# A decayed recurrence and routed attention on one core: small copies on ScalarE and GpSimd, and a new table of order, buffers and engines

## The chip, the cores and the metric

The kernel runs on 1 core of one Trainium2 chip. The metric is the device time in microseconds (us); lower is better. Engines are named as in the profile: PE is TensorE, DVE is VectorE, ACT is ScalarE, POOL is GpSimd, SP is SyncE, which issues every transfer (DMA) of this kernel.

## The reference

Four batches, 8 heads, 768 time steps, head width 48. A linear recurrence with a complex decay runs over time; its output, 384 wide per step, goes through four experts' causal attention, of which each step uses its two best.

```python
mag = np.sqrt(a_re * a_re + a_im * a_im)
scale = np.minimum(mag, 0.999) / (mag + 1e-06)
a_re_n, a_im_n = (a_re * scale, a_im * scale)
for t in range(S):
    new_re = ar * S_re - ai * S_im
    new_im = ar * S_im + ai * S_re
    kv = np.einsum('bhd,bhe->bhde', k[:, :, t], v[:, :, t])
    S_re, S_im = (new_re + kv, new_im)
    y[:, :, t] = np.einsum('bhd,bhde->bhe', q[:, :, t], S_re)
...
logits = x @ w_gate                      # x is y with its heads side by side
topk = np.argpartition(-logits, K, axis=-1)[..., :K]        # K = 2 of 4
w = np.exp(sel); w /= w.sum(-1, keepdims=True) + 1e-09
for e in range(E):
    q, k, v = x @ wq[e], x @ wk[e], x @ wv[e]
    scores = np.where(causal, -1e9, scale * (q @ k.transpose(0, 2, 1)))
    a = np.exp(scores - scores.max(-1, keepdims=True))
    a /= a.sum(-1, keepdims=True) + 1e-09
    ye = a @ v @ wo[e]
    out += mask[..., None] * w[:, :, kk:kk + 1] * ye        # for both chosen kk
```

## The kernel before, in words

The recurrence is done in chunks of 128 steps, 6 to a batch. Two chunks make a piece (256 steps), 3 to a batch, and the decay of a piece is worked out for all 384 features at once, in tiles of 128 partitions by 3 x 256 columns. For a piece, `logs` turns the magnitude into a running sum of logarithms (ACT logarithms and exponentials, DVE products and running sums, the "scans"), `atan` and `angles` do the same for the phase (its running sum goes on from the piece before through a small tile `carry`), `sincos` takes sine and cosine, and `products` multiplies q and k by them. For the very first piece, `groups` cuts this in three thirds of 128 x 256, so that each works while the next is loaded. `regroup` then moves the products by 10 transfers into `fm`, where the heads lie apart: heads 0 to 3 need the first 5 of the 10, heads 4 to 7 the last 5 or 6.

For each chunk PE makes the causal products `psc` (masked by DVE into `pts`), transposes k (`pk`, copied to `kts`), the state's increment `pu` (scaled into `tst`), and the output `yu` (copied to `x`). After two chunks `proj` multiplies x by the weights (`pp`), `vproj` makes values and logits (`pv`, `lg`), and `maxpass` takes row maxima (`pm`). When a batch's six chunks are done, `gate` picks the experts, `score` makes scores `pss` and their exponentials `pe` (POOL masks the diagonal blocks with affine_select), `av` multiplies by the values (`po`) and adds up the exponentials on DVE or POOL, `norm` divides (`dn`, `cb`, `ot`), and `wo` projects to the output (`pw`, `ob`). PE thus works on the scores of one batch while the recurrence of the next is prepared.

`record` lists all operations, 0 to 1875, without running them. The numbers below are places in that list. A table decides the rest: `ORDER` is the order in which they are issued, and so each engine's queue; `HOME` names operations that go to another engine than the one written (a ScalarE copy as `tensor_copy`, Square as a product, Abs as a bit mask, by `moved`); `ROOMS` says which buffer each tile gets; `FILL` puts so many filler matmuls ahead of an operation on PE. A filler multiplies the tile `keep` by itself into the bank that the operation will overwrite; it computes nothing and waits for nothing but `keep` and that bank. Line 860 is the filler's line, line 871 the line that issues all other operations, line 869 ACT's table load: ACT holds one set of functions at a time, one for sine and arctangent, one for logarithm and exponential, and a load stands wherever the order changes between them.

Operations that the prediction speaks of, all of batch 0: 7 makes `keep`; 33 to 35 load the three thirds of the first piece's decay, 118 and 119 the two halves of the second piece's (121 is the first ACT operation on it); 100 to 105 are the sines of the first piece, 106 to 117 its 12 products; 186 to 195 its `fm` transfers, 152 and 153 the decay of the third piece; 200 and 202 the two `psc` of the first chunk (heads 0 to 3 and 4 to 7), 197 and 199 its `kts` copies, 204 its `pu`; 221 to 223 the second chunk's `yu`; 228 and 231 the first two projections; 269 and 283 are third- and fourth-chunk work (`pu` and a `psc`).

```python
for i in ORDER or range(len(plan.ops)):
    if i in FILL:
...
        for _ in range(FILL[i]):
            nc.tensor.matmul(z, real(plan.busy), real(plan.busy)[:, None, :].to_broadcast([128, 4, 128]),
                             start=True, stop=True)
```

Of the kernel before, what the change touches and what calls it, by code (L numbers as in the profile page):

```python
# [26 lines left out]
C2 = 2 * C  # L27
# [15 lines left out]
HOME = {26: 'gpsimd',  # L43
 32: 'gpsimd',
 40: 'vector',
 48: 'vector',
 70: 'vector',
 89: 'vector',
 97: 'vector',
 124: 'vector',  # L50
 134: 'vector',
 145: 'vector',
 150: 'gpsimd',
 169: 'gpsimd',
 183: 'gpsimd',
 199: 'vector',
 208: 'vector',
 213: 'vector',
 220: 'gpsimd',
 287: 'gpsimd',  # L60
 296: 'vector',
 303: 'vector',
 340: 'gpsimd',
 353: 'vector',
 424: 'gpsimd',
 437: 'gpsimd',
 459: 'gpsimd',
 473: 'gpsimd',
 497: 'gpsimd',
# [3 lines left out]
 549: 'gpsimd',  # L73
 551: 'gpsimd',
 563: 'gpsimd',
 571: 'gpsimd',
 583: 'gpsimd',
# [4 lines left out]
 599: 'gpsimd',  # L82
 605: 'gpsimd',
 617: 'gpsimd',
 619: 'gpsimd',
 630: 'gpsimd',
 631: 'gpsimd',
 632: 'gpsimd',
 751: 'vector',
 779: 'vector',  # L90
 781: 'vector',
 788: 'gpsimd',
 867: 'gpsimd',
 880: 'gpsimd',
 907: 'gpsimd',
 926: 'gpsimd',
 943: 'gpsimd',
 945: 'gpsimd',
 953: 'gpsimd',
 960: 'vector',  # L100
 961: 'gpsimd',
 963: 'vector',
 966: 'vector',
 975: 'vector',
 985: 'gpsimd',
 996: 'vector',
 1013: 'gpsimd',
 1030: 'gpsimd',
 1031: 'gpsimd',
 1033: 'gpsimd',  # L110
 1039: 'gpsimd',
 1041: 'vector',
 1044: 'gpsimd',
 1046: 'gpsimd',
 1065: 'gpsimd',
 1067: 'gpsimd',
 1080: 'gpsimd',
 1109: 'vector',
 1116: 'gpsimd',
 1135: 'vector',  # L120
 1167: 'gpsimd',
 1174: 'vector',
 1176: 'vector',
 1183: 'gpsimd',
 1187: 'vector',
 1192: 'vector',
 1199: 'vector',
 1201: 'vector',
 1227: 'vector',
 1240: 'vector',  # L130
 1313: 'gpsimd',
 1320: 'gpsimd',
 1328: 'gpsimd',
 1337: 'gpsimd',
 1339: 'gpsimd',
 1345: 'gpsimd',
 1347: 'gpsimd',
 1354: 'vector',
 1367: 'gpsimd',
 1369: 'gpsimd',  # L140
 1374: 'gpsimd',
 1381: 'vector',
 1382: 'gpsimd',
 1387: 'gpsimd',
 1399: 'gpsimd',
 1409: 'gpsimd',
 1411: 'vector',
 1420: 'vector',
# [3 lines left out]
 1478: 'gpsimd',  # L152
 1479: 'gpsimd',
 1481: 'gpsimd',
 1493: 'gpsimd',
 1494: 'gpsimd',
 1495: 'gpsimd',
 1501: 'gpsimd',
 1512: 'vector',
# [6 lines left out]
 1564: 'gpsimd',  # L166
 1579: 'vector',
 1580: 'vector',
 1583: 'vector',
 1608: 'vector',  # L170
 1619: 'vector',
 1622: 'vector',
 1624: 'vector',
 1640: 'vector',
 1643: 'vector',
 1647: 'vector',
 1708: 'vector',
 1709: 'vector',
 1712: 'vector',
 1761: 'gpsimd',  # L180
 1763: 'gpsimd',
 1776: 'gpsimd',
 1835: 'gpsimd',
 1856: 'vector',
 1857: 'gpsimd'}

FILL = {202: 141, 204: 14, 206: 1, 210: 7, 357: 3, 406: 2, 1873: 4}

ROOMS = {'ab': [0, 1, 0, 1, 0, 1, 0, 1, 0, 1, 0, 1],
 'carry': [0, 3, 2, 3, 2, 1, 1, 3, 1, 2],  # L190
 'fm': [0, 1, 0, 1, 0, 1, 0, 1, 0, 1, 0, 1],
# [30 lines left out]

ORDER = [13, 35, 20, 0, 34, 14, 19, 33, 15, 6, 17, 118, 1, 2, 4, 18, 3, 5, 8, 119, 9, 12, 21, 120, 22, 67, 36, 68, 185, 52, 69, 53, 70, 154, 37, 54, 71, 7,
# [160 lines left out]
def record(ak, vk, w, out):  # L384
    p = Plan()
    V, G = "vector", "gpsimd"
# [4 lines left out]
    ab, fm, vt, xk, qka, v2, lgs, mrow, mx, ot = ({} for _ in range(10))  # L391
# [263 lines left out]
    def gate(b):  # L655
        lg = lgs[b]
# [273 lines left out]
```

## Time and profile before

| what | value |
|---|---|
| median of 3 runs (lowest, highest) | 414.89 us (413.98, 415.06) |
| the profiled execution | 413.87 us, its span 412.2 us |
| PE busy | 398.0 us, 97% of the span |
| DVE, ACT, POOL busy | 346.3 (84%), 280.3 (68%), 157.5 us (38%) |
| granted PE clock, mean | 0.996 of full speed |
| DMA | 53.40 MB moved, 130 GB/s in the mean |

The span runs from the first to the last instruction of one execution; 1.67 us of that execution's time lies around it. A busy PE may be busy with fillers. Queues of the engines run in order: an instruction that waits holds everything behind it on its engine.

### The profile page before, as it was taken

The page shows a single profiled execution, that of the slowest core. Times are in us where ns is not written, and L with a number is a line of the kernel's source. Part 1 is how long each engine was busy: PE and PEld are TensorE (multiplying, and loading weights), DVE is VectorE, ACT ScalarE, POOL GpSimd, SP SyncE. Part 2 cuts the span into 40 slices and gives each one's busy share as a digit, 9 for nine tenths or more (in the row PEclk, how much of TensorE's full clock was granted, in tenths as well). Part 3 has the DMA queues.
Part 4 walks back from the last instruction along what each step waited for, and adds up shares of the span by engine and source line. Part 5 has one row for each costly group of instructions (what it writes and reads, how often), then busy time and mean ns, then how long its engine had stood idle before and what let it go on. Part 6 is the DMA issues. An engine that isn't in the chain of part 4 may idle for free. (4 is left out here: it accounts for less than half of the span.)

```text
span 412.2 us, 9649 instructions
## 1 busy us (share of the span) xinstructions
PE 398.0 (97%) x3792; PEld 326.9 (79%) x3792; DVE 346.3 (84%) x738; ACT 280.3 (68%) x436; POOL 157.5 (38%) x146
## 2 busy tenths in 40 slices
PE   4999799999999999999999999999999999999996
PEld 1445579998888779989887789989779789887775
DVE  5997979999999999999999898798794556978751
ACT  6979788986898898879688999733533222124572
POOL 0002233559373444563263324640166634002440
PEclk9999989999999999999999999999999999999999
DMA  7767808875946506828424703628003510111002
GB/s 266 281 158 202 231 0 214 231 218 132 342 117 190 154 37 164 233 63 269 126 71 116 212 3 116 191 76 233 9 2 76 165 27 2 38 45 54 2 13 103
DMA packets 27261, 53.40 MB, mean 130 GB/s; under 512 B 3536, under 2 KB 7376, under 8 KB 27216
## 3 DMA queue, kind: packets, MB, share of 16 engines
q1 hardware_dynamic: 27216, 52.78, 44.2%
q8 instruction: 30, 0.49, 0.5%
q14 instruction: 15, 0.12, 0.1%
HBM read 26.74 MB, written 4.72 MB: 76 GB/s over the span
## 5 line engine op out<-in xcount | busy, mean ns | idle before, releaser
L871 POOL TENSOR_TENSOR qk<-qk,ab 128x768 f32<-128x768 f32 x20 | 40.0, 2011 | 64.2 <-DVE qk L871 49.1
L871 ACT ACTIVATE pe<-pss 128x1024 f32<-128x1024 f32 (+2 forms) x48 | 43.4, 915 | 26.0 <-PE pss L871 22.4
L871 POOL TENSOR_SCALAR_AFFINE_SELECT pe<-pe 128x256 f32<-128x256 f32 x48 | 25.3, 544 | 84.8 <-ACT pe L871 54.8
L871 PE MATMUL pp<-x,whi 128*128 128x256 f32 x288 | 55.6, 287 | 0.1
L871 PE MATMUL psc<-fm 96*128 96x128 f32 x384 | 52.1, 281 | 0.2
L871 PEld LDWEIGHTS psc<-fm 96*128 96x128 f32 x384 | 46.6, 192 | 3.2 <-issue 0.9
L871 ACT ACTIVATE ab<-ab 128x768 f32<-128x768 f32 (+1 forms) x61 | 45.8, 762 | 4.3 <-DVE ab L871 3.2
L871 PEld LDWEIGHTS pp<-x,whi 128*128 128x128 f32 x288 | 45.4, 189 | 1.5 <-issue 1.5
L871 ACT ACTIVATE qk<-qk 128x768 f32<-128x768 f32 (+3 forms) x64 | 43.1, 684 | 4.0 <-DVE qk L871 3.6
L871 PE MATMUL pss<-qka 64*128 64x256 f32 (+3 forms) x480 | 45.5, 301 | 0.1
L871 PE MATMUL po<-pe,v 128*64 128x256 f32 (+3 forms) x320 | 42.8, 395 | 0.8 <-POOL pe L871 0.8
L869 ACT ACT_TABLE_LOAD x33 | 42.3, 1283 | 1.3 <-PEq L919 0.8
L871 POOL TENSOR_TENSOR pe<-pe 128x512 f32<-128x512 f32 (+2 forms) x25 | 31.7, 1267 | 28.6 <-DVE pe L871 13.3
L860 PEld LDWEIGHTS <-keep 128*128 128x128 bf16 x172 | 17.2, 102 | 29.8 <-issue 6.8
L871 PEld LDWEIGHTS pss<-qka 64*128 64x128 f32 x480 | 35.7, 185 | 6.2 <-issue 2.4
L871 PE MATMUL pp<-x,wlo 128*128 128x256 f32 x144 | 40.3, 280 | 0.0
L860 PE MATMUL psc<-keep 128*128 128x512 bf16 x141 | 32.9, 398 | 6.0 <-DVE keep L871 6.0
L871 DVE TENSOR_TENSOR pts<-psc,keep 128x512 f32<-128x512 f32 x48 | 32.3, 682 | 5.3 <-PE yu L871 2.9
L871 POOL TENSOR_TENSOR qk<-qk 128x768 f32<-128x768 f32 x16 | 25.8, 1620 | 23.6 <-ACT qk L871 23.4
L871 DVE CUSTOM_DVE_ANT_0 junk<-pm,negm 128x128 bf16<-128x128 f32 (+3 forms) x64 | 31.1, 485 | 3.3 <-PE pm L871 2.1
L871 PEld LDWEIGHTS po<-pe,v 128*64 128x64 f32 x320 | 20.7, 136 | 14.9 <-issue 5.0
L871 PE MATMUL pv<-whi,x 128*128 128x260 f32 x144 | 31.1, 292 | 0.0
(121 smaller groups left out, 930.6 us busy)
## 6 DMA issues: line engine op xcount, KB each, us to landing
fm<-qk SPq DMA_DIRECT2D x72, 192.8 KB, 4.7
qk<-in_ak_dram SPq DMA_DIRECT2D x12, 768.0 KB, 5.7
ab<-in_ak_dram SPq DMA_DIRECT2D x22, 384.0 KB, 4.0
vt<-in_vk_dram SPq DMA_DIRECT2D x12, 512.0 KB, 5.9
out_dram<-ob SPq DMA_DIRECT2D x24, 192.0 KB, 1.9
fm<-qk SPq DMA_DIRECT2D x24, 128.5 KB, 4.1
x<-x SPq DMA_DIRECT2D x24, 96.0 KB, 3.0
fm<-qk SPq DMA_DIRECT2D x24, 64.2 KB, 4.2
```

The lines of the kernel that those rows point to most:

```text
L860: nc.tensor.matmul(z, real(plan.busy), real(plan.busy)[:, None, :].to_broadcast([128, 4, 128]), start=True, stop=True)
L869: nc.scalar.preload_act_table_set(need)
L871: getattr(getattr(nc, engine), name)(*a, **k)
```

## The change

Two lines of code move small copies that carry a result on: the end of a piece's phase (`carry`, 10 copies of 128 x 1 or 128 x 3) and the middle part of the gate's coefficients (`cft`, 4 copies of 24 x 128). Both were written for VectorE; they are now ScalarE copies, of which `HOME` sends two `carry` copies to GpSimd.

All four tables are new. `HOME` has other entries: besides the copies, 37 products, sums and splits go from POOL to DVE and 29 from DVE to POOL; copies out of PSUM and within SBUF change between DVE and ACT in both directions (`kts`: 10 from DVE to ACT, 3 back; `x`: 4 and 1). `ORDER` is another order throughout, and with it the number of ACT table loads is 29 (before: 33). `ROOMS` follows it. `FILL` has 185 fillers (before: 172): 130 (141) ahead of the first `psc`, 48 (22) more up to the second chunk's `pu`, and 7 (9) later.

```diff
-HOME = {26: 'gpsimd',
- 32: 'gpsimd',
+HOME = {32: 'gpsimd',
  40: 'vector',
- 48: 'vector',
+ 55: 'vector',
+ 63: 'gpsimd',
...
-FILL = {202: 141, 204: 14, 206: 1, 210: 7, 357: 3, 406: 2, 1873: 4}
+FILL = {200: 130, 202: 17, 204: 14, 206: 6, 218: 3, 221: 8, 288: 2, 406: 3, 1870: 2}
...
-ORDER = [13, 35, 20, 0, 34, 14, 19, 33, 15, 6, 17, 118, 1, 2, 4, 18, 3, 5, 8, 119, 9, 12, 21, 120, 22, 67, 36, 68, 185, 52, 69, 53, 70, 154, 37, 54, 71, 7,
+ORDER = [20, 33, 14, 19, 34, 0, 7, 35, 9, 6, 118, 119, 23, 36, 185, 154, 37, 38, 22, 52, 39, 53, 40, 120, 121, 4, 54, 250, 55, 41, 67, 42, 56, 2, 11, 68, 57,
...
         if k + 1 < NK:
             c = p.tile([128, 3], F32, "carry")[:, :len(js)]
-            p.put(V, "tensor_copy", c, A[:, :, C2 - 1])
+            p.copy(c, A[:, :, C2 - 1])
...
         p.tt(V, r, z, cft[:n], OP.subtract)
-        p.put(V, "tensor_copy", cft[32:32 + n], r)
+        p.copy(cft[32:32 + n], r)
```

First place: the start of DVE's queue, where `keep`, for which the first filler waits, is made. Before, 13 setup operations and three of the decay stood ahead of it:

```order
L871 TENSOR_SCALAR pickneg<-pickneg 128x6
L871 MEMSET col 128x1
L871 MEMSET cmask 128x2
L871 MEMSET negm 128x192
L871 TENSOR_SCALAR negm<-iota 128x128
L871 CAST pick<-ident 24x24
L871 TENSOR_TENSOR ab<-ab 128x256 x3
L871 TENSOR_SCALAR keep<-iota 128x128
```

and of the change, from the first row of the queue:

```order
L908 UNCONDITIONAL_BRANCH
L853 TENSOR_SCALAR keep<-iota 128x128
L853 TENSOR_SCALAR negm<-iota 128x128
L853 TENSOR_SCALAR ident<-iota 128x128
L853 TENSOR_TENSOR ab<-ab 128x256 x2
L853 MEMSET cmask 128x256
```

`keep` is now the first thing that DVE makes (POOL's `iota`, which it reads, has moved behind two small POOL operations).

Second place: the start of ACT's queue, `ab_63` and `qk_102` (`qk_84` in the change) being the first piece's tiles and `ab_80` (`ab_79`) the second piece's. Before, from its third operation:

```order
L871 ACTIVATE qk_102<-ab_63 128x256
L871 ACTIVATE ab_63<-qk_102 128x256
L871 ACTIVATE qk_102<-ab_63 128x256 x2
L871 ACTIVATE ab_63<-ab_63 128x256
L871 ACTIVATE ab_63<-qk_102 128x256
L871 ACTIVATE qk_102<-qk_102 128x256
L871 ACTIVATE qk_102<-ab_63 128x256
L871 ACTIVATE qk_102<-qk_102 128x256
L871 ACTIVATE qk_98<-ab_80 128x3x256
```

and of the change, from its first:

```order
L853 ACTIVATE qk_84<-ab_63 128x256
L853 ACTIVATE ab_63<-qk_84 128x256
L853 ACTIVATE qk_84<-ab_63 128x256
L853 ACTIVATE ab_63<-qk_84 128x256
L853 ACTIVATE qk_99<-ab_79 128x3x256
L853 ACTIVATE qk_84<-ab_63 128x256 x3
L853 ACTIVATE ab_63<-qk_84 128x256
```

The second piece's operation 121 stands after 4 ACT operations on the first piece instead of after 11.

Third place: DVE's queue from the first chunk's `pts` to the second chunk's. Before:

```order
L871 COPY kts<-pk 128x384
L871 SCALAR_TENSOR_TENSOR qk<-qk 128x3x256
L871 SCALAR_TENSOR_TENSOR ab<-col,carry,ab 128x256 x3
L871 SCALAR_TENSOR_TENSOR qk<-qk 128x3x256
L871 SCALAR_TENSOR_TENSOR qk<-cmask,qk 128x256 x3
L871 TENSOR_TENSOR ab<-ab 128x768
L871 SCALAR_TENSOR_TENSOR ab<-ab 128x768
L871 TENSOR_TENSOR tst<-pu,fm 96x384
L871 TENSOR_TENSOR pts<-psc,keep 128x512
L871 CAST x<-yu 128x4x128
L871 TENSOR_TENSOR pts<-psc,keep 128x512
L871 COPY kts<-pk 128x384
```

and of the change:

```order
L853 SCALAR_TENSOR_TENSOR qk<-qk 128x3x256
L853 MEMSET negm 128x192
L853 SCALAR_TENSOR_TENSOR qk<-cmask,qk 128x256 x3
L853 TENSOR_TENSOR ab<-ab 128x768
L853 TENSOR_TENSOR pts<-psc,keep 128x512
L853 TENSOR_TENSOR x<-yu,x 128x4x128
L853 TENSOR_TENSOR tst<-pu,fm 96x384
L853 SCALAR_TENSOR_TENSOR ab<-ab 128x768
L853 TENSOR_TENSOR qk<-qk 128x3x256
L853 TENSOR_TENSOR pts<-psc,keep 128x512
L853 SCALAR_TENSOR_TENSOR qk<-qk 128x3x256
L853 TENSOR_TENSOR wlo<-wst,whi 128x768
```

The two `kts` copies and the `x` copy have left DVE for ACT, and one `pts` and the state's `tst` stand ahead of the phase's `ab` operation instead of behind it.

## Rows read from the trace of the kernel before

**Rows 1.** The page's part 1: busy us, share of the span and instructions of each engine.

```profile
PE 398.0 (97%) x3792; PEld 326.9 (79%) x3792; DVE 346.3 (84%) x738; ACT 280.3 (68%) x436; POOL 157.5 (38%) x146
```

**Rows 2.** Stretches: length, busy us of PE, PEld, DVE, ACT, POOL, clock, DMA share, GB/s.

```profile
51.66:55.07 3.41, 3.41 (x13) 1.84 (x12) 1.52 (x3) 3.38 (x5) 0.94 (x1) 0.50 0.00 1
64.40:400.00 335.60, 333.74 (x3388) 287.93 (x3386) 288.34 (x620) 224.74 (x344) 144.30 (x131) 1.00 0.42 120
400.00:412.20 12.20, 8.67 (x59) 6.86 (x57) 3.48 (x8) 3.97 (x9) 1.90 (x3) 1.00 0.26 98
```

**Rows 3.** Timeline of PE and its weight loads: start, length, operation, [idle before].

```profile
6.04 32.89 PE L860 MATMUL psc<-keep 128*128 128x512 bf16 x141 [6.04 <-DVE keep L871]
...
10.71 27.73 PEld L860 LDWEIGHTS <-keep 128*128 128x128 bf16 x129 [0.28 <-issue]
...
38.77 1.95 PE L871 MATMUL psc<-fm 96*128 96x128 f32 x16
...
46.09 1.56 PE L871 MATMUL pu<-vt,kts 128*96 128x48 f32 x16 [0.34 <-ACT kts L871]
...
51.44 2.96 PE L860 MATMUL pk<-keep 128*128 128x512 bf16 x7 [1.94 <-DVE tst L871]
...
55.38 1.09 PE L871 MATMUL yu<-pts,vt 128*64 128x128 f32 x16
...
64.44 0.36 PE L871 MATMUL pp<-x,whi 128*128 128x256 f32 x1
```

**Rows 4.** Timeline of ACT in the first piece.

```profile
6.12 0.72 ACT L871 ACTIVATE qk<-ab 128x256 f32<-128x256 f32 x2 [0.74 <-DMA ab<-in_ak_dram]
...
10.05 1.32 ACT L871 ACTIVATE qk<-qk 128x256 f32<-128x256 f32 x4
11.39 1.28 ACT L869 ACT_TABLE_LOAD   x1
12.69 1.76 ACT L871 ACTIVATE ab<-ab 128x256 f32<-128x256 f32 x4
...
22.42 0.89 ACT L871 ACTIVATE ab<-ab,col 128x256 f32<-128x256 f32 x2
```

**Rows 5.** SP's timeline, and transfers by issue window: count, KB each, us to landing.

```profile
2.32 0.47 SPq L871 DMA_DIRECT2D ab<-in_ak_dram  x1
...
ab<-in_ak_dram SPq DMA_DIRECT2D x1, 384.0 KB, 5.0
...
26.53 5.25 SPq L871 DMA_DIRECT2D fm<-qk  x7
...
fm<-qk SPq DMA_DIRECT2D x2, 192.8 KB, 3.6
...
fm<-qk SPq DMA_DIRECT2D x2, 192.8 KB, 6.7
```

**Rows 6.** Timeline of DVE: its start, the products of two pieces, the second chunk.

```profile
1.51 0.22 DVE L871 TENSOR_SCALAR ident<-iota 128x128 f32<-128x128 f32 x1
...
22.78 2.76 DVE L871 TENSOR_TENSOR qk<-qk,ab 128x256 f32<-128x256 f32 x8
...
36.14 2.69 DVE L871 TENSOR_TENSOR qk<-qk,ab 128x768 f32<-128x768 f32 x3 [0.65 <-ACT ab L871]
...
48.62 2.30 DVE L871 SCALAR_TENSOR_TENSOR ab<-ab 128x768 f32<-128x768 f32 x1
...
51.31 0.67 DVE L871 TENSOR_TENSOR pts<-psc,keep 128x512 f32<-128x512 f32 x1
```

**Rows 7.** ACT's timeline from the second piece on.

```profile
24.72 1.73 ACT L871 ACTIVATE qk<-qk 128x768 f32<-128x768 f32 x2
26.36 1.56 ACT L871 ACTIVATE whi<-wst 128x768 fp32r<-128x768 f32 x2
...
45.57 0.47 ACT L871 ACTIVATE kts<-pk 128x384 f32<-128x384 f32 x1
```

**Rows 8.** Waits of PE from 60 us on: us in total, times, longest.

```profile
PE po L871 <- POOL pe L871: 0.8, 1, 0.8
```

More of the change, by code (lines that the diff above doesn't have):

```diff
@@ L41 @@
  (((1, 2, 3), (1, 2, 3, 4, 5)), ((1, 2, 3), (1, 2, 3, 4, 5))), (((1, 2, 3), (1, 2, 3, 4, 5)), ((1, 2, 3), (1, 2, 3, 4, 5))))
-HOME = {26: 'gpsimd',
- 32: 'gpsimd',
+HOME = {32: 'gpsimd',
  40: 'vector',
- 48: 'vector',
+ 55: 'vector',
+ 63: 'gpsimd',
  70: 'vector',
- 89: 'vector',
- 97: 'vector',
+ 78: 'gpsimd',
+ 87: 'gpsimd',
+ 92: 'vector',
+ 99: 'vector',
  124: 'vector',
- 134: 'vector',
+ 143: 'vector',
  145: 'vector',
- 150: 'gpsimd',
+ 168: 'gpsimd',
  169: 'gpsimd',
  183: 'gpsimd',
- 199: 'vector',
- 208: 'vector',
- 213: 'vector',
  220: 'gpsimd',
  287: 'gpsimd',
- 296: 'vector',
- 303: 'vector',
  340: 'gpsimd',
  353: 'vector',
+ 365: 'vector',
+ 419: 'gpsimd',
  424: 'gpsimd',
- 437: 'gpsimd',
+ 449: 'gpsimd',
  459: 'gpsimd',
- 473: 'gpsimd',
- 497: 'gpsimd',
+ 491: 'gpsimd',
+ 495: 'gpsimd',
  503: 'gpsimd',
@@ L72 @@
  513: 'gpsimd',
- 549: 'gpsimd',
+ 527: 'vector',
+ 548: 'gpsimd',
  551: 'gpsimd',
- 563: 'gpsimd',
+ 565: 'gpsimd',
  571: 'gpsimd',
+ 582: 'gpsimd',
  583: 'gpsimd',
@@ L81 @@
  598: 'gpsimd',
- 599: 'gpsimd',
  605: 'gpsimd',
  617: 'gpsimd',
- 619: 'gpsimd',
- 630: 'gpsimd',
+ 624: 'gpsimd',
  631: 'gpsimd',
  632: 'gpsimd',
- 751: 'vector',
- 779: 'vector',
- 781: 'vector',
+ 668: 'gpsimd',
+ 680: 'vector',
+ 735: 'gpsimd',
+ 754: 'vector',
  788: 'gpsimd',
[L93 to L96, printed above, removed]
+ 816: 'vector',
+ 919: 'gpsimd',
+ 921: 'gpsimd',
  943: 'gpsimd',
  945: 'gpsimd',
+ 951: 'gpsimd',
  953: 'gpsimd',
- 960: 'vector',
  961: 'gpsimd',
  963: 'vector',
- 966: 'vector',
- 975: 'vector',
  985: 'gpsimd',
- 996: 'vector',
- 1013: 'gpsimd',
+ 997: 'gpsimd',
+ 1019: 'gpsimd',
  1030: 'gpsimd',
- 1031: 'gpsimd',
  1033: 'gpsimd',
[L111 to L114, printed above, removed]
+ 1045: 'gpsimd',
  1065: 'gpsimd',
  1067: 'gpsimd',
+ 1077: 'gpsimd',
+ 1078: 'gpsimd',
+ 1079: 'gpsimd',
  1080: 'gpsimd',
- 1109: 'vector',
- 1116: 'gpsimd',
+ 1095: 'vector',
+ 1131: 'vector',
  1135: 'vector',
  1167: 'gpsimd',
- 1174: 'vector',
- 1176: 'vector',
  1183: 'gpsimd',
- 1187: 'vector',
- 1192: 'vector',
- 1199: 'vector',
+ 1195: 'vector',
  1201: 'vector',
- 1227: 'vector',
- 1240: 'vector',
- 1313: 'gpsimd',
+ 1236: 'gpsimd',
+ 1249: 'vector',
+ 1260: 'vector',
+ 1261: 'vector',
+ 1263: 'vector',
+ 1264: 'vector',
+ 1315: 'gpsimd',
  1320: 'gpsimd',
  1328: 'gpsimd',
+ 1333: 'gpsimd',
  1337: 'gpsimd',
[L135 to L142, printed above, removed]
- 1382: 'gpsimd',
[L144 to L148, printed above, removed]
+ 1382: 'gpsimd',
+ 1423: 'vector',
  1433: 'gpsimd',
@@ L151 @@
  1447: 'gpsimd',
- 1478: 'gpsimd',
- 1479: 'gpsimd',
- 1481: 'gpsimd',
+ 1452: 'gpsimd',
+ 1459: 'gpsimd',
+ 1467: 'gpsimd',
+ 1486: 'gpsimd',
+ 1487: 'gpsimd',
+ 1492: 'gpsimd',
  1493: 'gpsimd',
- 1494: 'gpsimd',
  1495: 'gpsimd',
- 1501: 'gpsimd',
- 1512: 'vector',
+ 1512: 'gpsimd',
+ 1513: 'gpsimd',
  1515: 'gpsimd',
@@ L165 @@
  1555: 'vector',
- 1564: 'gpsimd',
+ 1557: 'vector',
+ 1573: 'vector',
  1579: 'vector',
- 1580: 'vector',
  1583: 'vector',
- 1608: 'vector',
- 1619: 'vector',
+ 1606: 'vector',
+ 1615: 'gpsimd',
  1622: 'vector',
[L173 to L179, printed above, removed]
+ 1631: 'gpsimd',
+ 1684: 'gpsimd',
+ 1711: 'vector',
  1761: 'gpsimd',
  1763: 'gpsimd',
[L182 to L185, printed above, removed]
-FILL = {202: 141, 204: 14, 206: 1, 210: 7, 357: 3, 406: 2, 1873: 4}
+ 1768: 'gpsimd',
+ 1781: 'gpsimd',
+ 1803: 'gpsimd'}
+FILL = {200: 130, 202: 17, 204: 14, 206: 6, 218: 3, 221: 8, 288: 2, 406: 3, 1870: 2}
 ROOMS = {'ab': [0, 1, 0, 1, 0, 1, 0, 1, 0, 1, 0, 1],
- 'carry': [0, 3, 2, 3, 2, 1, 1, 3, 1, 2],
- 'fm': [0, 1, 0, 1, 0, 1, 0, 1, 0, 1, 0, 1],
+ 'carry': [3, 2, 0, 0, 3, 0, 2, 1, 3, 2],
+ 'fm': [1, 0, 1, 0, 1, 0, 1, 0, 1, 0, 1, 0],
  'gcf': [0, 0, 0, 0],
@@ L194 @@
  'grk': [0, 0, 0, 0],
- 'kts': [0, 0, 0, 1, 1, 0, 0, 1, 1, 0, 0, 0, 0, 0, 1, 0, 0, 0, 0, 1, 0, 1, 1, 0],
- 'lg': [1, 1, 0, 0],
- 'mpart': [0, 1, 1, 0, 1, 0, 0, 1, 0, 1, 1, 0, 0, 1, 0, 1],
+ 'kts': [0, 0, 0, 1, 0, 0, 1, 0, 1, 1, 0, 0, 0, 1, 0, 1, 1, 0, 1, 0, 1, 0, 1, 0],
+ 'lg': [1, 0, 1, 1],
+ 'mpart': [0, 1, 1, 0, 0, 1, 0, 1, 0, 1, 0, 1, 1, 0, 1, 0],
  'mrow': [0, 0, 0, 0, 0, 0, 0, 0],
[1 row of a table removed]
[1 row of a table added]
  'ot0': [0, 0, 0, 0],
  'ot1': [0, 0, 0, 0],
[10 rows of a table removed]
[10 rows of a table added]
          0, 1],
- 'pts': [1, 0, 1, 0, 0, 1, 1, 0, 1, 0, 1, 0, 1, 0, 0, 1, 0, 1, 1, 0, 1, 0, 1, 0, 0, 1, 1, 0, 0, 1, 0, 1, 0, 1, 1, 0, 1, 0, 1, 0, 0, 1, 1, 0, 1, 0, 1,
+ 'pts': [0, 1, 0, 1, 1, 0, 1, 0, 1, 0, 0, 1, 0, 1, 1, 0, 1, 0, 0, 1, 0, 1, 0, 1, 0, 1, 1, 0, 1, 0, 1, 0, 0, 1, 0, 1, 0, 1, 1, 0, 0, 1, 1, 0, 1, 0, 1,
          0],
- 'qka': [0, 1, 0, 1, 0, 1, 0, 1],
- 'r': [0, 1, 0, 1, 1, 0, 1, 0, 1, 1, 1, 1, 1, 1, 0, 1, 1],
- 'tst': [0, 0, 1, 0, 0, 0, 1, 1, 0, 1, 1, 1, 0, 1, 0, 0, 1, 1, 0, 1],
[4 rows of a table removed]
-ORDER = [13, 35, 20, 0, 34, 14, 19, 33, 15, 6, 17, 118, 1, 2, 4, 18, 3, 5, 8, 119, 9, 12, 21, 120, 22, 67, 36, 68, 185, 52, 69, 53, 70, 154, 37, 54, 71, 7,
[68 rows of a table removed]
+ 'qka': [1, 0, 1, 0, 1, 0, 1, 0],
+ 'r': [0, 1, 1, 0, 1, 1, 0, 1, 1, 1, 1, 0, 1, 1, 0, 1, 1],
+ 'tst': [1, 1, 0, 1, 1, 1, 1, 1, 0, 1, 1, 0, 0, 1, 0, 0, 1, 1, 0, 1],
[4 rows of a table added]
+ORDER = [20, 33, 14, 19, 34, 0, 7, 35, 9, 6, 118, 119, 23, 36, 185, 154, 37, 38, 22, 52, 39, 53, 40, 120, 121, 4, 54, 250, 55, 41, 67, 42, 56, 2, 11, 68, 57,
[68 rows of a table added]
 class View:
```

164 rows, old and new, of tables (ORDER, ROOMS) are left out of this document.

## Prediction

> **What bounds the kernel now.** I read the busy times first. PE is busy 398.0 us [rows 1] of a 412.2 us span, 97%; DVE has 84% and the others less, so only what lets PE start earlier, wait less or do less can shorten the run. The table of stretches says where PE waits: from 64.4 to 400 us it is busy 333.74 of 335.60 us, 1.86 us idle in a third of a millisecond, and in the last 12.2 us it is busy 8.67 [rows 2]. Only the prologue is left, where busy is not the same as useful: PE waits 6.04 us for `keep`, then runs 141 fillers until 38.93, the first `psc` follows at 38.77 (the ends of a pipelined engine overlap a little), 14 and 7 more fillers stand further on, and the projections start at 64.44 [rows 3]. What sets 64.44 is therefore not PE but the chain behind the fillers: ACT's logarithms and sines, DVE's products, the `fm` transfers, then the first two chunks on PE, ACT and DVE in turn. Two losses are seen in it. Before the second chunk PE idles 1.94 us until DVE's `tst`, and after that the granted clock is 0.50, the lower of the two levels, for 3.41 us [rows 2, 3], so that 7 fillers take 2.96 us where 129 at full clock took 27.73, 0.215 each. And the fillers end a little late: the last `fm` issue ends at 31.78 and the slow transfers of that kind land 6.7 us after their issue [rows 5], by about 37.8 for heads 4 to 7, hence about 1 us before PE has got through its fillers.
>
> Ahead of that, ACT sets the pace: it stands 0.74 us for the first load, and its last sine ends at 23.31 (22.42 + 0.89) [rows 4]; DVE's last first-piece product ends at 25.54 (22.78 + 2.76) [rows 6]; ACT then goes on with the second piece until 46.04, where the first chunk's `kts` copy is done [rows 7]. In the steady part the longest wait of PE is a single one, 0.8 us for a mask of POOL's [rows 8].
>
> **The change, part by part.** The run profiled is 413.87 us, its span 412.2; it lies 1.02 us under the median of 414.89. I work out a difference on its own time and put that on the median.
>
> *Start of the fillers.* `keep` becomes DVE's first operation. An operation of that size on the same `iota` ran on DVE at 1.51 and took 0.22 [rows 6]; POOL makes `iota` two small operations later (bounded by 0.22 each from that row, below by nothing). The first filler starts at about 1.9 instead of 6.04, at latest 2.2. The first 11 of them took 4.67 us (6.04 to 10.71), 0.425 each, the rest 0.215 [rows 3]; 130 then end at 1.9 + 11 x 0.425 + 119 x 0.215 = 32.2, before 38.9. So this itself brings nothing: it lets PE meet the data instead of being behind it.
>
> *First piece.* On ACT, operation 121 now stands behind 4 operations instead of 11. Its transfer was issued at 2.32 and took 5.0 us [rows 5], so ACT stands until 7.3, and the 7 operations that it jumped over wait for it, with all of DVE's scans and products behind them. From there 29 operations of 128 x 256 at 0.33, two of 768 columns at 0.82, four small ones at about 0.1 and three table loads at 1.30 [rows 4, 7] after the 0.8 of operation 121 itself give 8.1 + 9.6 + 1.6 + 0.4 + 3.9 = 23.6: the last sine ends 0.3 later than before (bounds: nothing, if the load comes earlier; 1 us if the scans between them add up). Last product about 26.0 to 26.5. SP issues `fm` transfers at 0.75 each (7 in 5.25) [rows 5]; heads 0 to 3 have theirs issued by 27.3 and need 3.6 to 6.7 us: 31 to 34. Heads 4 to 7 have the last one issued at 31.45 and, with 6.0 to 6.7, landed by 37.5 to 38.2. With fillers ending at 32.2 the first `psc` starts near 32.8 and its second half, behind 17 fillers (3.7 us), near 38.2; before, both were done at 40.72, now at 39.2. That is 1.5 us early.
>
> *Second piece on ACT.* What limits the first chunk's `pu` is `kts`, now queued on ACT behind the whole second piece: 19 operations of 768 columns x 0.82, five table loads x 1.29 and about 1.3 for `kts`, `x` and `carry`, 23.3 us from 23.7: done at 47.0, where before it was 46.04 [rows 7]. Two of those five loads are new. So `pu` starts 0.9 us **later** than its 46.09.
>
> The table loads can be weighed against a rule. The row has 1.28 for a load, with the next operation 1.30 after the load's start [rows 4]. The Trainium skill (page "ScalarE: Activation LUTs", section "What ACT_TABLE_LOAD costs") says that each switch costs about 2.66 us, as a drain of 1.38 comes on top of the load's 1.28. By the page, two more loads would put `pu` another 2.8 us late (rival E). The trace here disagrees: the gap from the operation before to the one after is that of the load alone, and I take the trace's.
>
> *Second chunk.* After `pu` (1.4 us) before: `psc` for both halves, 1.94 idle, 7 slow fillers, `pk`, and `yu` at 55.38 [rows 3]. The idle time came from DVE: `tst` stood behind a phase operation of 2.30 us at 48.62 [rows 6]. Now `tst` (about 0.5 us, from 0.67 for a tile of 512 columns) stands ahead of it, right behind `pu` at 48.4 to 48.9; then the phase operation (0.9 by the products' row, 2.69/3, or 2.30 as here), another of 0.9 and `pts` 0.67 [rows 6]: 51.4 to 52.8. PE has `pk` and half a `psc` (0.82 + 0.98, to 50.2) and 8 fillers (1.72) to 51.9. I take the lower value, as the row's 2.30 is more than twice that of its neighbours: `yu` at 51.9 instead of 55.38, with no idle time long enough to be seen and no half clock. Of these 3.5 us, 1.94 is the idle time, 1.5 the half clock (2.96 - 7 x 0.215 = 1.46).
>
> *To the projections.* Behind `yu` the new order has 2.0 us of `yu`, two half `psc` (2.0), three transposes (1.6 in all), `pu` twice (2.8), 3 fillers (0.65), another half `psc` (0.98) and the third chunk's `yu` (1.95), 11.9 in all: the first projection at about 64.0 instead of 64.44. But 269 and 283, 1.4 + 0.98 us of it, are done by then, and were not before. PE's lead at that point is 0.4 + 2.4 = 2.8 us.
>
> *Later.* The 7 later fillers instead of 9 save 0.4; the waits that remain in a new order of the same kind I price at 0.6 (a dozen of 0.05, from 1.86 us in 335.6 [rows 2]). The carried copies, 14 of them, and the net shift between POOL and DVE take about 3 us from DVE (84% busy) and 3 from or to engines with 68% and 38%: nothing on PE's path, as the work beside PE hides it; without that cover a `carry` copy costs at most a 256-column operation, 0.33 [rows 4], once a piece, since it stands between one piece's angles and the next, and a queue behind a sine waits for it. At the tail the last `ot` loses its POOL step, 0 to 0.7; two fillers fewer are in the 0.4. Sum: 2.8 + 0.4 - 0.6 = **2.6 us less**: profiled run 411.3, median 412.3.
>
> **Rivals.**
> *A, the first `fm` half lands late.* At 6.7 instead of 5.5 heads 0 to 3 come at 34, and PE idles from 32.2, nearly the 1.94 us after which this trace has the clock at 0.50 [rows 2, 3]. The 17 fillers then take 0.425 each, 3.6 us more, and as the data for heads 4 to 7 are there at 38, about 2.2 to 2.9 of the gain goes: 414.5 to 414.9, no change. For it: 1.8 us is all the room that the estimate has. [...]
> *B, the lead is given back.* PE comes to the batch's gate and scores earlier, and the second batch's recurrence on ACT and DVE, whose work has not shrunk, is as late as ever; with DVE at 84% that costs what was won: 414.9. Against it: DVE and ACT are idle in 16 and 32% of the span, and 1.86 us of waiting in 335.60 [rows 2] says that PE is not led by them.
> *C, slower.* Around the scores, POOL's masks and DVE's sums stand in another order, between more DVE work (37 operations came, 29 went). Each time that a sum or mask is not there when `po` or `dn` wants it PE waits; the only row of that kind has 0.8 [rows 8]. The new order decides it: four such waits eat the gain, six make 4.8 - 2.6 = 2.2 us more, 417.1. For it: the order is new over 335 us and 1.86 us of waiting leaves little to win but much to lose.
> *D, the copies do nothing and the tables differ only in noise* gives the time of B.
> *E, a table load holds ACT longer than its row.* If the operation behind a load came 2.7 us after the load's start instead of 1.30 [rows 4], two more loads would put `kts`, `pu` and all behind them 2.8 us later, and -2.6 becomes +0.2: 415.1. The row itself speaks against it, so that it gets 0.01, in B's share. (It is the Trainium skill's rule on table loads, above.)
>
> **How the numbers follow.** Forecast 0.55 (its own range 410.4 to 413.6: -4.5 if the tail gives 0.7 and `fm` lands at once, -1.3 if the phase operation takes 2.30). A 0.14, B with D and E 0.13, C 0.18. The smallest difference told from none is 0.3%, 1.24 us: faster is under 413.65, slower over 416.13. The forecast is nearly all faster (0.52), with some of A (0.03): 0.55. Most of A, B, D and E and the edge of the forecast are the same: 0.27. C is slower: 0.18. The range reaches from the forecast's lower part, 410.0, to 416.5, which holds A, B and the mild part of C, and leaves out little more than 0.15.
>
> **What would show it.** First filler at 1.9; first `psc` near 33 and its second half near 38; `pu` near 47.0, later than before; the second chunk's `yu` near 52 with clock 1.00 at 50 to 55; the projections at 64 with 269 and 283 behind them; PE's idle time from 64 to 400 near 2 us. The prediction is wrong where the clock falls at 32 to 38 (A), where that idle time is above 4 us (C), or where `pu` starts after 49 us (E).

## The result, and the profile after

The changed kernel takes 418.0 us (median of 4, 416.47 to 421.91) against 414.5 for the kernel before: ratio 1.0122, 95% interval 1.0078 to 1.0167. It is **slower by 1.2%**, where 412.3 was forecast and 416.5 was the upper end of the range. The profiled execution took 416.95 us.

The page of the changed kernel, span and busy times [rows 1]:

```profile
span 415.2 us, 9660 instructions
...
PE 399.9 (96%) x3805; PEld 325.1 (78%) x3805; DVE 345.3 (83%) x713; ACT 284.1 (68%) x456; POOL 142.0 (34%) x147
```

Its timeline of PE over the start (columns as in [rows 3]):

```profile
1.86 30.94 PE L842 MATMUL psc<-keep 128*128 128x512 bf16 x130 [1.86 <-DVE keep L853]
32.63 1.06 PE L853 MATMUL psc<-fm 96*128 96x128 f32 x8
...
37.20 1.05 PE L853 MATMUL psc<-fm 96*128 96x128 f32 x8
...
40.87 1.09 PE L853 MATMUL yu<-pts,vt 128*64 128x128 f32 x16 [0.99 <-DVE pts L853]
...
46.57 1.56 PE L853 MATMUL pu<-vt,kts 128*96 128x48 f32 x16 [0.17 <-ACT kts L853]
...
51.31 1.09 PE L853 MATMUL yu<-pts,vt 128*64 128x128 f32 x16 [0.18 <-DVE pts L853]
...
63.29 0.36 PE L853 MATMUL pp<-x,whi 128*128 128x256 f32 x1
```

The start went as worked out: fillers from 1.86, the second chunk's `yu` at 51.31 instead of 55.38, the projections at 63.29 instead of 64.44, with 269 and 283 (1.4 + 0.98 us) already done. At that point PE is 1.15 + 2.38 = 3.5 us ahead; 2.8 had been forecast.

The same profile in two stretches from there on (columns as in [rows 2]), and PE's waits in the first of them (us in total, times, longest; compare [rows 8]):

```profile
63.29:400.00 336.71, 328.42 (x3332) 280.72 (x3330) 283.28 (x596) 219.85 (x349) 133.00 (x131) 1.00 0.40 114
400.00:415.20 15.20, 11.76 (x90) 9.22 (x87) 6.33 (x13) 7.21 (x15) 0.74 (x1) 1.00 0.22 79
```

```profile
PE pm L853 <- DVE mx L853: 2.7, 1, 2.7
PE pp L853 <- DVE qka L853: 1.3, 1, 1.3
PE pk L853 <- DVE pts L853: 1.2, 1, 1.2
PE dn L853 <- DVE lg L853: 1.0, 1, 1.0
PE dn L853 <- POOL pe L853: 0.9, 1, 0.9
PE pmr L853 <- DVE mx L853: 0.4, 1, 0.4
PE pk L853 <- DVE wst L853: 0.3, 1, 0.3
```

PE is idle for 336.71 - 328.42 = 8.29 us there; before it was 1.86 [rows 2]. That is the loss: -3.5 at the start, +6.4 of waits, -0.4 for two fillers fewer make +2.5 of the 3.0 by which the spans differ. The other 0.5 lies spread in PE's busy time.

Ahead of each of the three longest waits, 5.2 us together, stands the same event, seen when DVE's timeline is laid beside POOL's. First DVE, then POOL, at the same three moments:

```profile
85.57 3.96 DVE L853 SCALAR_TENSOR_TENSOR ab<-ab 128x768 f32<-128x768 f32 x1
...
140.11 2.33 DVE L853 SCALAR_TENSOR_TENSOR ab<-ab 128x768 f32<-128x768 f32 x1
...
168.50 2.65 DVE L853 TENSOR_TENSOR qk<-qk,ab 128x768 f32<-128x768 f32 x1
```

```profile
85.66 3.05 POOL L853 TENSOR_TENSOR qk<-qk 128x768 f32<-128x768 f32 x2
...
140.07 1.55 POOL L853 TENSOR_TENSOR qk<-qk 128x768 f32<-128x768 f32 x1
...
168.48 1.86 POOL L853 TENSOR_TENSOR qk<-qk,ab 128x768 f32<-128x768 f32 x1 [1.52 <-ACT ab L853]
```

Each of the DVE operations reads two operands in SBUF and takes 0.95 at other places. Here each begins within 0.1 us of a POOL product that also reads two SBUF operands, and ends 0.8 us after the POOL product (at the first place two, back to back) is done: 85.66 + 3.05 = 88.71, and DVE is done at 89.53. So it did nothing until POOL had finished. The excess is 3.0 + 1.4 + 1.7 = 6.1 us of DVE, and what stands behind on its queue is what PE waits for: the row maxima `mx`, then `pts`, then `qka`. The chain of work that ended last shows the first stall as "issue", time in which the engine waited for nothing that the profile shows:

```profile
85.65 0.07 DVE ab L853
85.72 3.73 issue
89.45 0.41 DVE junk L853
```

DVE operations with one operand in PSUM that run beside POOL's products for 0.2 us or more (`pts` 29 times, `x<-yu,x` 14, `qka<-pp,qka` 12) show nothing of the kind: all of them lie within 0.1 us of their usual time.

### The profile page after: what moved, and what is told of

Same layout as the page of the kernel before. It is cut to its first block, busy times and chain, and to the rows that moved or that the text cites. A ratio compares the mean times of both kernels' runs of the same rounds, so it can differ in the third digit from the quotient of the medians.

```text
span 415.2 us, 9660 instructions
## 1 busy us (share of the span) xinstructions
PE 399.9 (96%) x3805; PEld 325.1 (78%) x3805; DVE 345.3 (83%) x713; ACT 284.1 (68%) x456; POOL 142.0 (34%) x147
## 4 chain that ended last, share of the span: by engine, by line
PE 59%; ACT 18%; DVE 10%; DMA 5%; issue 4%; POOL 2%; SPq 1%; DVEq 0%; ACTq 0%; POOLq 0%
PE pss L853 9%; PE pp L853 8%; PE po L853 7%; PE psc L853 6%; ACT ab L853 6%; ACT qk L853 6%; PE pw L853 6%; PE yu L853 6%; PE pv L853 5%; PE pu L853 4%; ACT L851 4%; PE pm L853 3%; DMA ab<-in_ak_dram 3%; PE pk L853 3%; PE dn L853 2%
## 5 line engine op out<-in xcount | busy, mean ns | idle before, releaser
L853 ACT ACTIVATE ab<-ab 128x768 f32<-128x768 f32 (+1 forms) x58 | 44.0, 770 | 4.7 <-DVE ab L853 3.1
L853 POOL TENSOR_SCALAR_AFFINE_SELECT pe<-pe 128x256 f32<-128x256 f32 x48 | 23.1, 498 | 69.8 <-ACT pe L853 61.4
L853 POOL TENSOR_TENSOR qk<-qk,ab 128x768 f32<-128x768 f32 x19 | 34.6, 1837 | 27.7 <-DVE qk L853 15.3
L853 PE MATMUL po<-pe,v 128*64 128x256 f32 (+3 forms) x320 | 43.7, 395 | 0.0
L842 PEld LDWEIGHTS <-keep 128*128 128x128 bf16 x185 | 18.4, 101 | 24.0 <-issue 3.7
L842 PE MATMUL psc<-keep 128*128 128x512 bf16 x147 | 34.8, 401 | 1.9 <-DVE keep L853 1.9
L853 DVE TENSOR_TENSOR pe<-pe 128x512 f32<-128x512 f32 (+2 forms) x43 | 29.1, 676 | 8.9 <-POOL pe L853 6.8
L853 PEld LDWEIGHTS pu<-vt,kts 128*96 128x96 f32 x320 | 29.1, 165 | 3.7 <-ACT kts L853 1.7
L853 DVE TENSOR_TENSOR qk<-qk,ab 128x768 f32<-128x768 f32 (+1 forms) x37 | 28.9, 822 | 3.0 <-ACT ab L853 1.9
L853 PE MATMUL pu<-vt,kts 128*96 128x48 f32 x320 | 30.4, 248 | 0.5 <-ACT kts L853 0.5
```

The costliest lines, as they stand in the source:

```text
L853: getattr(getattr(nc, engine), name)(*a, **k)
```

## The experiments

Three theories. **1**: DVE and POOL exclude each other while both read SBUF as above; three near ties (the two begin within 0.1 us of each other) make the loss. **2**: DVE is full, so whatever PE gains at the start is given back. **3**: the carried copies on ScalarE hold up the next piece. Each kernel but the last two is the change with a few lines added behind its tables; `behind(after, ...)` moves operations in `ORDER` to a place behind another. Medians are of 6 or 12 runs, ratios to the kernel before on the same chip. What was expected is quoted as written ahead of each run.

**a0_change_again**: the change itself, as the base.

> The changed kernel as it is, as the base of the runs beside it. Its first four runs lay between 416.5 and 421.9 us, with a mean clock of 0.988 to 1.0. All theories expect about 417 to 418 us, 1.2% over the kernel before; where the profiled run is one with a lower clock, its trace shows behind which wait of PE the clock falls.

Measured 418.57 us, ratio 1.0106 (1.0072 to 1.0140). Its twelve runs reach from 413.98 to 422.59, and the mean granted clock falls on the whole as they get longer, from 0.999 in the shortest to 0.980 in the longest. This profiled run has nearly the same waits as the first (2.89 us for `mx` at 91.56), but here the clock falls behind the first of them. Two stretches of it:

```profile
88.00:92.90 4.90, 2.01 (x17) 1.32 (x14) 4.90 (x9) 2.61 (x3) 1.41 (x1) 1.00 0.56 139
92.90:96.31 3.41, 3.41 (x19) 3.41 (x18) 3.06 (x10) 2.52 (x4) 2.90 (x2) 0.52 0.20 55
```

PE is busy for 2.01 of 4.90 us, and then runs for 3.41 us at 0.52; at the lower level half of that, 1.7 us, is lost. So a wait in the middle of the kernel can cost its own length and 1.7 us more. At a mean clock of 0.998 or above, six runs of before lie between 411.2 and 412.3 and three of the change between 414.0 and 416.6: without the clock the change is still about 3.7 us slower.

**a1_pool_to_dve**: the four POOL products of the three near ties run on DVE.

```diff
+HOME.update({585: 'vector', 583: 'vector', 997: 'vector', 1045: 'vector'})
```

> The four POOL operations beside which three DVE operations stood for 3.96, 2.33 and 2.65 us (instead of 0.94) now run on DVE. Theory 1 (DVE and POOL exclude each other when both read two SBUF operands; three near ties cost DVE 6.1 us, and the waits of PE right behind them are 2.73, 1.21 and 1.27 us): DVE gets 6.1 us back and 4 x 0.95 = 3.8 us of work; PE's three waits shrink to 1 us in all, the time falls by 2.5 to 4 us against the change, to 414 to 415. Theory 2 (DVE is full between 20 and 240 us, so PE's early start is given back whatever stands where): 3.8 us more work on DVE makes it slower by 1 to 4 us. Theory 3 (the carried copies on ScalarE hold up the phase of the next piece): no change.

Measured 413.92 us, ratio 1.0013 (0.9986 to 1.0041): by the two ratios 3.8 us less than a0 on the same chip (by the two medians 4.7), though DVE got 3.8 us of work more (and lost the 6.1 us of standing). DVE's phase operation is back at 0.95. PE's three waits are now 0.62, 0.92 and 0.32 us (the 1.6 below holds another of 0.96, at 94.94), 1.9 in all where 1 had been expected. At the second place little is gained, as the product that left POOL now stands ahead of `qka` on DVE:

```profile
86.58 0.95 DVE L855 SCALAR_TENSOR_TENSOR ab<-ab 128x768 f32<-128x768 f32 x1
```

```profile
PE dn L855 <- POOL pe L855: 2.0, 1, 2.0
PE pm L855 <- DVE mx L855: 1.6, 2, 1.0
PE pk L855 <- DVE qka L855: 0.9, 1, 0.9
...
PE pp L855 <- DVE qka L855: 0.3, 1, 0.3
```

Theory 2 had the sign wrong. Part of the gain is the clock: at a mean clock of 0.998 or above, a0's three runs have a median of 415.4 us, a1's eight 413.5 and the six of the kernel before 411.8. So at a like clock the ties are worth about 2 us, and a1 is still 1.7 us slower than the kernel before. The move also changed DVE's queue, so the next two runs put the clash back without the work.

**d1_pool_two_inputs**: a1, and two idle POOL products on a scratch tile at the first place.

```diff
+if i == 204:
+    dum = pools[0].tile([128, 2, 512], F32, name="dum", tag="pe_1", bufs=1)
+    nc.gpsimd.memset(dum, 0.0)
+if i == 585:
+    for _ in range(2):
+        nc.gpsimd.tensor_tensor(dum[:, 0], dum[:, 0], dum[:, 1], op=OP.mult)
```

> As the run with the four operations on DVE (a1), and besides, where the first near tie was, POOL does two idle products of 512 columns that read two SBUF operands (a scratch tile, nobody waits for them; the estimate is 1.29 us each, as the changed kernel's other products of that size). Theory 1: DVE's phase operation there takes 0.94 + 2.6 = 3.5 us again, PE's wait for the row maxima grows from 0.62 to about 2.7, and the time from 1.001 of the kernel before to about 1.008 (with the half clock that such a wait brings in some runs). Theory 2, and whoever puts the loss on the order of the queues: nobody waits for these products, so nothing changes.

Measured 416.77 us, ratio 1.0083 (1.0053 to 1.0114). DVE, POOL and PE's wait:

```profile
87.50 2.18 DVE L861 SCALAR_TENSOR_TENSOR ab<-ab 128x768 f32<-128x768 f32 x1
```

```profile
87.60 3.21 POOL L851 TENSOR_TENSOR dum<-dum 128x512 f32<-128x512 f32 x2
```

```profile
PE pm L861 <- DVE mx L861: 2.7, 1, 2.7
```

Nobody waits for these products, no queue of DVE, ACT or PE is altered, and PE's wait is back at 2.7 us and the time at the forecast ratio. That is theory 1, and neither of the others. The stall is shorter than expected, 2.18 (3.5): POOL's two products lie 0.08 us apart here, and DVE came in between them; the second product and the next DVE product (1.68 us) then paid.

**d2_pool_one_input**: the same with five POOL operations that read one SBUF operand.

```diff
-    for _ in range(2):
-        nc.gpsimd.tensor_tensor(dum[:, 0], dum[:, 0], dum[:, 1], op=OP.mult)
+    for _ in range(5):
+        nc.gpsimd.tensor_scalar(dum[:, 0], dum[:, 0], 1.0, 0.0, op0=OP.mult, op1=OP.add)
```

> The same with five idle POOL operations of 512 columns that read one SBUF operand (a factor and a sum by constants), about 0.6 us each, 3 us in all. Theory 1: DVE and POOL do not exclude each other here: the phase operation stays at 0.95 us, PE's wait at 0.6, the time at 1.001 of the kernel before. A theory in which any POOL work beside DVE costs DVE time expects the stall and about 1.008, as with two operands.

Measured 414.47 us, ratio 1.0037 (1.0010 to 1.0065), PE's first wait 0.66. The time lies near the expected 1.001, but the reason given did not hold. POOL's five operations, minimum, median and maximum in ns, by the view of the tile:

```profile
L851 POOL TENSOR_SCALAR dum<-dum x5: 621/1202/1224, 86.4 to 90.4; 128x512 f32<-128x512 f32 x5
```

POOL takes 0.62 us where it is alone and 1.2 beside each of DVE's two-operand operations, so the two exclude each other with one operand on POOL as well. Here DVE came first, and a POOL operation of 0.6 us, in its turn, held DVE's later ones up by 0.1 and 0.3 only. What counts is who is first and how long the holder holds.

**a2_dve_later**: nothing changes engines; DVE's three operations are issued a few places later.

```diff
+behind(249, 592, 593)
+behind(732, 1006, 1025)
+behind(748, 1044)
```

> The three DVE operations that met a POOL operation are issued a few places later, behind the row maxima, the masked scores and the copy for which PE waited; nothing leaves or enters DVE. Theory 1: the three waits of PE (5.2 us) go, or all but about 1 us; 4 us less than the change, 413 to 414, no slower than the kernel before. Theory 2: DVE has as much to do as ever and something else is late by as much: no change, 417 to 418. Theory 3: no change.

Measured 418.92 us, ratio 1.0121 (1.0090 to 1.0152): a miss. The first clash is still there, 2.89 us on DVE at 87.67. The maxima are early now, but ScalarE's next operation, on the same data, waits for DVE and holds ScalarE's queue, in which the copy `qka` stands that PE wants. ACT's timeline, then PE's:

```profile
90.59 0.85 ACT L863 ACTIVATE ab<-ab 128x768 f32<-128x768 f32 x1 [3.35 <-DVE ab L863]
...
95.06 0.57 ACT L863 ACTIVATE qka<-pp 128x512 fp32r<-128x512 f32 x1
```

```profile
95.69 0.56 PE L863 MATMUL pm<-qka 64*128 64x512 f32 x2 [3.13 <-ACT qka L863]
```

The wait of 2.7 us on DVE became one of 3.1 on ACT. The other two clashes are gone, 3.1 us of DVE, yet PE's idle time after the first projection is 6.1 us against 6.9 in a0 and the time is no better. A stalled operation costs through every queue that depends on it, and its own length does not say how much.

**a3_late_start**: 14 more fillers ahead of the first `psc`.

```diff
+FILL[200] += 14
```

> The change with 14 more fillers ahead of the first scores, 3.0 us, which takes away the lead that PE had at the first projection (2.9 us). Theory 1: PE sets the time but where a near tie stands; it ends 1 to 3 us later than the change, 419 to 421. Theory 2: DVE sets it and PE only waits less behind: no change, 417 to 418, with PE's waits from 64 to 400 us 3 us shorter than the change's 8.3.

Measured 422.63 us, ratio 1.0214 (1.0178 to 1.0250), 4 us more than a0 and above what either theory expected. PE's waits after the first projection did not shrink (8.8 us of 336.7, against 6.9 in a0), which speaks against theory 2. But the test is weaker than meant: about half of the 3.0 us fell into the wait ahead of `yu` (1.52 us in a0, none here), and the first projection came only 0.55 us later than in a0 (64.55 against 64.00). The rest of the 4 us is waits and 10.2 us at half clock instead of 6.8.

**a4_copies_on_dve**: a1 with the 14 carried copies back on VectorE, which undoes the two changed lines of code.

```diff
+for i in (91, 86, 96, 142, 556, 590, 1004, 1038, 1452, 1486, 404, 852, 1300, 1748):
+    HOME[i] = 'vector'
```

> As a1, with the 14 carried copies (10 carry, 4 of the gate) back on VectorE, as the kernel before had them: the two changed lines of code undone by the table. Theory 1 and the prediction: these copies cost nothing on either engine, 1.001 of the kernel before within 0.4%. Theory 3 (a carried copy waits on ScalarE behind what is queued there and holds the next piece): faster than a1 by 1 to 3 us, 0.995.

Measured 415.39 us, ratio 1.0044 (1.0018 to 1.0071), against 1.0013 (0.9986 to 1.0041) for a1: not faster, so theory 3 falls. The two intervals overlap, so that a gain of 0.3% by the copies on ScalarE is not shown.

**a5_four_waits, a6_three_waits, a7_first_on_pool**: a1 mended further. a5:

```diff
+HOME.update({943: 'vector', 951: 'vector'})
+behind(297, 585, 583)
+behind(718, 997)
+behind(748, 1045)
```

a6 leaves 951 on POOL and has `FILL[206] += 5`; a7 is a6 with 585 and 583 on POOL and these two lines in place of the first `behind`:

```diff
+behind(249, 592, 593)
+behind(299, 620, 595)
```

> As a1, with what PE still waits for taken out: the first two products stand behind the maxima and the copy, the third and fourth behind the copies that PE wants, and two sums of exponentials go from POOL, where four stood in a row, to DVE, which was idle there. Theory 1: PE's waits of 0.62, 0.96, 0.92, 0.32 and 1.99 us shrink to about 1 us in all: 3 to 4 us less than a1, 2 more where the half clock goes with them, 408 to 411 us, 0.99 of the kernel before. Theory 2: DVE is full, no gain: 1.00.

> As the run a5, but only one of the two sums goes to DVE (the other had held up a copy for which PE then waited 1.67 us), and 5 more fillers ahead of the first chunk's output, where PE stands idle for 1.0 to 1.7 us and, in a5's profiled run, the clock then fell. Theory 1: the wait at 275 us is under 0.5, the clock stays at 1.00 over the start in most runs, 1 to 3 us less than a5: 0.995 of the kernel before. Theory 2: no gain, 1.00.

> As a6, but the first two products stay on POOL, DVE's phase operation is issued behind the maxima, and on ScalarE the copy for which PE then waited (3.13 us in a2) stands ahead of the arctangent and the second sine. Theory 1: DVE's phase operation stands for about 2.9 us as in a2, but PE no longer waits for what is behind it: PE's waits around 90 us are under 1 us, and the time is that of a6 or 1 us less, 0.993 to 0.996. If the stall itself costs, wherever it stands, the wait comes back elsewhere and the time is 1.005.

Measured 413.98 (1.0016, 0.9992 to 1.0040), 413.69 (1.0000, 0.9975 to 1.0025) and 413.90 us (1.0005, 0.9984 to 1.0027): no version beats the kernel before, and none of the gains that were expected came. Each new order also deals new clashes: in a7 DVE stands for 2.55 us at the first place, as meant, but also for 2.02 at 98.15 and 1.65 at 108.34, and PE's waits at 94.32 and 104.16, 1.48 and 1.04 us, are above the 1 us expected. In a5 the 1.99 us at 276 became 1.67 for an `x` copy pushed back by the sum that had moved to DVE, and a gap of 1.65 us at 42 was followed by a fall of the clock:

```profile
44.60:48.01 3.41, 3.41 (x14) 1.79 (x14) 3.41 (x7) 3.41 (x6) 0.00 (x0) 0.56 1.06 290
```

In a6 PE's idle time from the first projection on (64.01) is down to 3.1 us in 336.7, and the profiled run still takes 412.5 of span, with one such fall behind 0.72 and 0.98 us of waits.

**b1_before_later, b2_before_copy_first**: the kernel before, whose 2.30 us at 48.62 [rows 6] was such a clash too. POOL's timeline of the kernel before:

```profile
48.52 1.58 POOL L871 TENSOR_TENSOR qk<-qk 128x768 f32<-128x768 f32 x1 [8.01 <-ACT qk L871]
```

That kernel has another clash, late in its run, which costs PE no wait: this DVE operation takes 0.54 us at other places, and the next wait of PE that shows is one of 0.07 us at 378. DVE, then POOL:

```profile
323.25 1.69 DVE L871 TENSOR_TENSOR tst<-wst,fm 96x384 f32<-96x384 f32 x1
```

```profile
323.25 1.28 POOL L871 TENSOR_TENSOR ot<-r,ot 128x512 fp32r<-128x512 f32 x1
```

b1:

```diff
+HOME[26] = 'vector'
+behind(215, 177, 178, 26)
```

b2 moves ScalarE's copy 211 in front as well:

```diff
-behind(215, 177, 178, 26)
+behind(215, 211, 177, 178, 26)
```

> The kernel before, not the change, with its own near tie taken out: DVE's phase operation that stood for 2.30 us beside a POOL product at 48.62 is issued behind the state's scaling and both masked scores, and the POOL product after that (a split of weights) runs on DVE. Theory 1 (two SBUF operands on both engines exclude each other, and what is queued behind is late): PE's idle 1.94 us and the half clock behind it (1.46 us) go, the second chunk's output starts at 52 instead of 55.4, and the kernel is 2 to 3.4 us faster, 0.993 of the kernel before. Theory 2 (DVE sets the time, a start gained is given back): 1.00, since DVE gets 0.9 us more work and no less.

> As b1 (the kernel before without its first near tie), and the copy of the transposed k for which PE then stood 1.74 us moves on ScalarE ahead of the phase operation that waits for DVE; it is ready at 52.1 and ScalarE idle until 52.8. Theory 1, with the clock: the 1.74 us go and in most runs also the half clock that followed such a gap (b1 lay at 413.3 in ten of twelve runs and at 411.9 in the two with full clock): 410 to 411.5 us, 0.993 of the kernel before. Theory 2 (a start gained is given back to DVE, which has 84% to do): as b1, 0.998.

Measured 413.27 us for both, ratios 0.9981 (0.9963 to 0.9999) and 0.9998 (0.9975 to 1.0022). In b1 the operation takes 0.95 and the second chunk's `yu` starts at 52.10, as expected, but PE then waits for ScalarE's `kts`, and in b2, where that is early, for DVE's `wst`. One row of PE's timeline from b1, one from b2:

```profile
57.07 1.56 PE L880 MATMUL pu<-vt,kts 128*96 128x48 f32 x16 [1.74 <-ACT kts L880]
```

```profile
58.07 0.88 PE L880 MATMUL pk<-ident,fm 96*128 96x96 f32 x8 [1.83 <-DVE wst L880]
```

The profiled spans are 410.0 and 409.7 instead of 412.2. The earlier start (first projection at 62.71 and 61.33 instead of 64.44) is kept to the end, in b1 whole and in b2 2.5 of 3.1 us, which theory 2 denies. Yet the medians gain 0.2% at most, far from theory 1's 0.993, since in most runs of both the mean clock is 0.991 to 0.996: a gap of 1.7 to 1.8 us is still there, only elsewhere. The shorter spans are mostly the clock as well, for the profiled run of the kernel before had 0.996 and these two 1.000 and 0.998. At 0.998 or above, the kernel before takes 411.1 to 412.2 us on b1's chip and b1 411.8 and 411.9, no gain; on b2's chip it takes 411.5 to 411.8 and b2 410.9 to 411.5.

## Why the prediction was wrong

**Right.** PE as the bound, and the whole start: first filler 1.9 forecast and 1.86 measured, first `psc` 32.8 and 32.63 (partly by luck, as the fillers ahead of it ended at 32.80 and not at 32.2), its second half 38.2 and 37.20, `pu` 47.0 and 46.57 (later than before, as worked out), `yu` 51.9 and 51.31 with the clock at 1.00, the first projection 64.0 and 63.29. The table loads cost what the row said: `kts` was not late, so rival E is out. The copies cost nothing that a4 could show.

**The step that failed** is the one headed *Later*: "the waits that remain in a new order of the same kind I price at 0.6", and the work that moves between POOL and DVE is "nothing on PE's path, as the work beside PE hides it". Measured, PE waits 6.4 us more than before, and 8.3 in all is past the 4 us that the prediction had set as the sign of being wrong. Its sizes were off as well (POOL's busy time fell by 15.5 us, not by about 3), but no wait was worked out from them. The operations that moved were counted by the load of the engines, where they weigh little, and the new order by a flat price; what both did was to change which DVE operation begins beside which POOL operation. Three began together, and DVE stood 6.1 us longer than its work takes, at places where its queue is full and PE waits for what is behind. At the first and longest place nothing had moved: 583 and 585 ran on POOL and 592 on DVE before as well, and the order alone brought them together. At the other two, 997 and 1045 had come to POOL. a1 (3.8 us less without these ties) and d1 (the first wait back at 2.7 us with idle products) show it; for the second and third place alone there is the trace and a1, which takes all three away at once. The price of 0.6 would have been too low without the ties too: a1 still waits for 5.6 us.

**The sign was on record.** The row of 2.30 us at 48.62 was taken for a bound and put aside because it was "more than twice that of its neighbours". Why it was so long was not asked. POOL's product of 48.52 to 50.10 beside it would have told. The Trainium skill (page "SBUF — State Buffer", section "Who interferes with whom") states that a DVE instruction with two SBUF inputs contends with a GpSimd instruction that reads SBUF, and that the one issued first holds the shared ports while the other blocks. The traces here agree: 3.96 us on DVE beside two POOL products of 3.05 together, and d2's 1.2 instead of 0.62 us on POOL's side. The prediction did not weigh this rule.

**The rivals.** C ended on the right side, 417.1, by the right kind of sum (several waits, each near a microsecond), but at the wrong place: of 8.29 us only the 0.9 at `dn` for POOL's `pe` is a wait that it named, so that its nearness to 418.0 is mostly luck. B, the lead given back because DVE's work has not shrunk, is not what happened: a2 freed 3.1 us of DVE and gained nothing, and in the profiled runs of b1 and b2 an earlier start lasted. A did not occur in the profiled run; the 0.99 us ahead of `yu` at 40.87 is a wait for DVE's `pts`, not for `fm`. In a1's run, with the same start, PE did wait for `fm`, 0.20 and 0.76 us up to 33.74, and the clock did not fall there. (A's sum is off: 2.9 us taken from a gain of 2.6 gives 415.2, not 414.9. Nothing hangs on it.) The clock, which A allowed for at the start only, adds to the loss behind the later waits.

**What stays open.** After the three ties are taken out, 5.6 us of waits remain in a1, and they offset its lead of the start. What makes them was not worked out for each. a5 and a7 mostly moved them (4.8 and 5.4 us); a6 brought them down to 3.1 us, and its median gained nothing clear of the noise. Why the clock falls after one gap and not after another like it (2.73 us in the first profile of the change, 2.89 in a0) is not settled by these runs.

## What to carry to other kernels

Where work moves between VectorE and GpSimd, or the order of either queue changes, lay the two timelines side by side and mark the operations that read SBUF on both, on VectorE those with two SBUF operands: a tie there stops one engine for the length of the other's operation, and the profile names no releaser for it (the row is long, and at two of the three places here the chain has "issue"). What it costs depends on who waits behind: one of 1.1 us extra in the kernel before cost PE no wait. Look up each row that is much longer than its neighbours before using it as a bound. A start gained is worth nothing if it brings gaps of a microsecond or more further on, since each can cost its length and 1.7 us of half clock.

## What the runs showed of the hardware

Back-to-back POOL products did not let DVE in between them: 3.05 us in one piece at 85.66, where the second began before the first's end was recorded, while in d1 a gap of 0.08 us was enough. In these traces about 0.1 us decided who came first: POOL won where it began 0.01 us after the end of DVE's operation before (85.65 and 85.66), DVE where POOL began 0.13 us after it (86.23 and 86.36 in d2). And one program on one chip spread from 413.98 to 420.06 us in ten of a0's twelve runs, with mean clocks from 1.000 down to 0.988: waits that look alike in two profiles differ in what follows them.
